# The first four attention steps of an opening: reciprocals on 72 columns, spread back by fp32 matmuls, in a new order

## The chip, the cores and the metric

The kernel runs on one core of one Trainium2 chip. The metric is the device time of one execution in microseconds (us), taken as the median of several runs. The engines are called by the names of the profile: PE (TensorE, matmuls), PEld (its weight loads), DVE (VectorE), ACT (ScalarE), POOL (GpSimd) and SP (SyncE, which issues DMAs).

## What is computed

Sliding-window attention over 8 batches of 8 heads, 576 positions, head size 64, and then a two-layer feed-forward network on all 4608 tokens.

```python
scores = q @ k.T / sqrt(64);  scores = where(|i - j| <= 32, scores, -1e9)
attn = softmax(scores);       x = (attn @ v)            # heads joined: 4608 x 512
h = x @ w_in                                            # 512 -> 2048
out = maximum(0.01 * h, h) @ w_out                      # 2048 -> 512
```

Inputs and output are float32; the matmuls run on bfloat16 copies.

## The kernel before

Attention is cut into 64 steps. Step i is batch i // 8, half (i // 4) % 2 of the positions (288 queries) and head pair i % 4: two heads lie in partitions 0 to 63 and 64 to 127. One step goes through these helpers:

- `score(i)`: PE multiplies keys and queries block by block into the PSUM tile `ps` (columns 224 to 799).
- `exps(i)`: ACT takes the exponential of `ps` into `e` (bfloat16, 576 columns). There is no subtraction of a maximum.
- `masked(i, eng)`: `eng` multiplies by the window's mask into `prob`.
- `sums(i)`: PE multiplies by `ones_bd`, a block matrix of ones, so that each of the 64 rows of a head holds the same sum of probabilities for each of the 288 queries, in the PSUM tile `s`.
- `inverse(i)`: DVE takes the reciprocal of `s` (128 x 288, float32) into SBUF.
- `product(i)`: PE multiplies values and probabilities into the PSUM tile `x`.
- `scaled(i)`: DVE multiplies `x` by the reciprocal into `xT`, the transposed input of the feed-forward network.

The feed-forward network follows group by group (a group is 288 tokens, that is, four steps). `h_tile`, `h_open`, `h_chunk` and `h_first` compute 128 rows of the hidden layer (L401), ACT applies the leaky rectifier into `gT` (L412), and `o_tile` multiplies by `w_out` (L459) and stores 128 tokens.

PSUM is full: four slots of the pool `mmps` (transposes and feed-forward tiles share them), two banks for `ps`, one for `s` and one for `x`.

The order of the instructions on each engine is the order in which the program issues them; each engine runs its own list in order, and the framework adds the waits that data and buffers need. From step 8 on, a planner (`spend`, `due`, `SECOND`) puts attention steps between the matmuls of the feed-forward network. The opening, which is the first batch (steps 0 to 7) and the hidden tiles of its first group, is an order written out by hand (L524 to L649). In it the keys and queries are transposed by PE (`transpose_first`) and copied out of PSUM by `evict_first`; `value_first` casts the first values; `spread` copies the window mask into place, `fill` zeroes the columns of `ps` that no block writes, and `keep_busy` issues matmuls of zeros into columns 0 to 223 of `ps`. The weights `w_in` and `w_out` and the second batch's keys and queries come by DMAs that POOL issues (`load_w_in`, `load_w_out`, `load_first`), which also cast them. After the opening come `h_first(1)`, the other hidden tiles of group 1 (64 matmuls in all), and then the first output tile, ahead of which the planner's first entry transposes the second batch's first keys (`second_keys(0)`, `second_keys(1)`).

Before the change the first steps run as: `masked(0)`, `masked(1)` on DVE and the other six masks on POOL; every `inverse` on 288 columns; `h_chunk(0)` to `h_chunk(2)` (12 matmuls of the first four hidden tiles) stand before or beside `sums(4)`.

Of the kernel before, what the change touches and what calls it, by code (L numbers as in the profile page):

```python
# [16 lines left out]
def kernel(  # L17
# [91 lines left out]
    def load_v(b, p, engs=(nc.sync, nc.sync)):  # L109

        cast = engs[0] is nc.gpsimd
        if not cast:
            vf[b, p] = fload.tile([128, NB, D], FP32, name=f"vf{p}")
        for a, r in enumerate(HEADS):
# [14 lines left out]
    ones_bd = const.tile([128, 128], BF16)  # L129


    zero = const.tile([128, 1], BF16)

    WIN = [
        [((0, 0, 48), (2, 48, 64), (4, 112, 32)), ((1, 16, 64), (3, 80, 64))],
# [41 lines left out]
    nc.vector.memset(zero, 0.0)  # L177
# [24 lines left out]
    def transpose_first(b, p, which):  # L202

        src = (q0b, k0b)[which == "k"]
        tp = mmps.tile([128, ROW, 64], BF16, name="tp", tag="mm")
        for c in range(ROW):
            for r in HEADS:
                nc.tensor.transpose(tp[r, c], src[r, p, c], ident[r, r])  # L208
        trans[b, p, which] = tp.rearrange("p c i -> p i c")

    def evict_first(b, p, which, eng):
        if which == "q":
            if b not in qT:
                qT[b] = attn.tile([128, NPAIR, S], BF16, name="qT")
            to = qT[b][:, p]
        else:
            to = kTs[b, p] = kt.tile([128, S], BF16, name="kT")
        copy_to(eng, to.rearrange("p (i c) -> p i c", c=ROW), trans.pop((b, p, which)))

    def value_first(b, p, eng):  # L220
        copy_to(eng, v0b[:, p], vf[b, p])

    def fill(eng):
        eng.memset(ps[:, 512:512 + HALF], 0.0)
# [48 lines left out]
    def score(i):  # L273
        b, hf, p = where(i)
        if b == 0:
            by_n = ps[:, P0:P0 + 2 * HALF].rearrange("p (n t) -> p n t", n=2)
            for n_, blocks in enumerate(WIN[hf]):
                for blk, i0, n in blocks:
                    lo, hi = 2 * i0, 2 * (i0 + n)
                    for r in HEADS:  # L280
                        nc.tensor.matmul(  # L281
                            by_n[r, n_, lo:hi], kTs[b, p][r, 64 * blk:64 * blk + 64],
                            qT[b][r, p, hf * HALF + lo:hf * HALF + hi], start=True, stop=True,
                        )
        elif b < NATURAL:
            by_n = ps[:, P0:P0 + 2 * HALF].rearrange("p (n t) -> p n t", n=2)
            for n_, blocks in enumerate(WIN[hf]):
                for blk, i0, n in blocks:
                    lo, hi = 2 * i0, 2 * (i0 + n)
                    nc.tensor.matmul(  # L290
                        by_n[:, n_, lo:hi], kbd[b % 2][:, p, blk],
                        qT[b][:, p, hf * HALF + lo:hf * HALF + hi], start=True, stop=True,
                    )
        else:
            by_c = qT[b][:, p].rearrange("p (c i) -> p c i", c=2)
            for n_, blocks in enumerate(WIN[hf]):
                for blk, i0, n in blocks:
                    nc.tensor.matmul(  # L298
                        ps_v[:, n_, :, i0:i0 + n], kbd[b % 2][:, p, blk],
                        by_c[:, :, hf * EVEN + i0:hf * EVEN + i0 + n], start=True, stop=True,  # L300
                    )
        if b > 0:
            exps(i)
            masked(i, nc.vector if i in ON_DVE else nc.gpsimd)

    def exps(i):
        e = attn.tile([128, 2 * HALF], BF16, name="e")
        nc.scalar.activation(out=e, in_=ps[:, P0:P0 + 2 * HALF], func=AF.Exp, scale=scale)  # L308
        probs[i] = e

    def masked(i, eng):
        b, hf, p = where(i)
        e = probs[i]
        pr = prob[:, i % NPROB]
        allowed = mask_first[hf] if b < NATURAL else mask[hf].rearrange("p n c i -> p n (c i)")
        eng.tensor_mul(  # L316
            pr.rearrange("p n c i -> p n (c i)"), e.rearrange("p (n t) -> p n t", n=2), allowed,
        )
        probs[i] = [pr, None, None, None]

    def join(i):
# [4 lines left out]
        nc.vector.tensor_add(both, pr[:, 0], pr[:, 1])  # L326
        probs[i][1] = both

    def sums(i):

        b, hf, p = where(i)
        pr, both = probs[i][:2]
        s = xps.tile([128, HALF], FP32, name="s")
        if both is not None:
            nc.tensor.matmul(s, ones_bd, both, start=True, stop=True)  # L335
        else:
            for n in range(2):
                nc.tensor.matmul(
                    s, ones_bd, pr[:, n].rearrange("p c i -> p (c i)"),
                    start=(n == 0), stop=(n == 1),  # L340
                )
        probs[i][2] = s
        if b > 0:
            inverse(i)

    def inverse(i):
        r = recip.tile([128, HALF], FP32, name="r")
        nc.vector.reciprocal(r, probs[i][2])  # L348
        probs[i][2] = r

    def product(i):

# [73 lines left out]
    def h_close(f):  # L426
        h_out(0, f, opened.pop(f))
# [39 lines left out]
    def keep_busy(t, lo, n, start=False):  # L467


        for _ in range(n):  # L470
            nc.tensor.matmul(
                t[:, lo:lo + 224], ones_bd, busy, start=start, stop=False,
                skip_group_check=True,
            )
# [48 lines left out]

    V, G, A = nc.vector, nc.gpsimd, nc.scalar  # L524
    qT[0] = attn.tile([128, NPAIR, S], BF16, name="qT")
    keep_busy(ps, 0, 14, True)
    fill(V)
    transpose_first(0, 0, "k")
    evict_first(0, 0, "k", V)
    transpose_first(0, 0, "q")  # L530
    evict_first(0, 0, "q", A)
    transpose_first(0, 1, "k")
    score(0)
    evict_first(0, 1, "k", V)
    spread(A, GAP + 32, 2)
    load_v(0, 1, (G, G))
    transpose_first(0, 1, "q")
    exps(0)
    value_first(0, 0, V)
    transpose_first(0, 2, "k")  # L540
    evict_first(0, 1, "q", A)
    spread(V, 0, 3)
    masked(0, V)
    load_v(0, 2, (G, G))
    transpose_first(0, 2, "q")
    evict_first(0, 2, "k", V)
    sums(0)
    evict_first(0, 2, "q", A)
    score(1)
    inverse(0)  # L550
    transpose_first(0, 3, "k")
    exps(1)
    load_v(0, 3, (G, G))
    transpose_first(0, 3, "q")
    evict_first(0, 3, "k", A)
    score(2)
    product(0)
    evict_first(0, 3, "q", A)
    load_w_in(0, 512)
    masked(1, V)  # L560
    exps(2)
    scaled(0)
    sums(1)
    load_w_in(512, 1024)
    score(3)
    inverse(1)
    product(1)
    masked(2, G)
    exps(3)
    score(4)  # L570
    masked(3, G)
    exps(4)
    scaled(1)
    sums(2)
    product(2)
    inverse(2)
    score(5)
    load_w_in(1024, 1536)
    exps(5)
    masked(4, G)  # L580
    score(6)
    scaled(2)
    sums(3)
    h_chunk(0)
    load_w_in(1536, 2048)
    exps(6)
    inverse(3)
    h_chunk(1)
    masked(5, G)
    score(7)  # L590
    product(3)
    h_chunk(2)
    load_w_out(0)
    scaled(3)
    sums(4)
    exps(7)
    h_chunk(3)
    inverse(4)
    masked(7, G)
    product(4)  # L600
    h_close(0)
    h_close(1)
    h_open(4)
    load_w_out(1)
    h_close(2)
    h_open(5)
    scaled(4)
    h_close(4)
    sums(5)
    masked(6, G)  # L610
    h_open(6)
    h_close(3)
    inverse(5)
    h_close(5)
    h_open(7)
    h_close(6)
    product(5)
    load_w_out(2)
    h_close(7)
    h_open(8)  # L620
    h_open(9)
    load_w_out(3)
    h_close(8)
    scaled(5)
    sums(6)
    h_close(9)
    h_open(10)
# [4 lines left out]
    inverse(6)  # L632
    product(6)
    h_close(10)
    h_open(11)
    h_open(12)
    h_close(11)
    h_open(13)
    h_close(12)
    scaled(6)  # L640
    sums(7)
    h_close(13)
    h_open(14)
    inverse(7)
    h_open(15)
    h_close(14)
    product(7)
# [122 lines left out]
```

## Time and profile before

| what | value |
|---|---|
| runs | 317.68, 317.73, 318.78 us; median 317.73 |
| profiled execution | 319.02 us; span from its first to its last instruction 317.3 us |
| mean granted PE clock | 0.984 |
| busy | PE 306.0 (96%), DVE 218.9 (69%), POOL 187.7 (59%), ACT 167.5 (53%), PEld 204.6 (64%) |
| moved by DMA | 46.09 MB, mean 145 GB/s |
| 64 reciprocals on DVE (L348) | 125.2 us, 1956 ns each |
| hidden layer matmuls (L401) | 135.0 us, 1024 of them |
| output matmuls (L459) | 129.5 us |

Busy time is the time in which an engine has at least one instruction running; matmuls are pipelined, so the duration of one is longer than the distance from one to the next. In a timeline a line is a run of like instructions: start, length, engine, source line, operation, tiles, shapes, count, and in brackets the idle time before it with what ended it.

### The profile page before, as it was taken

How to read it: one execution, taken by the hardware profiler on the slowest of the kernel's cores; microseconds unless marked ns; L12 is line 12 of the kernel's file. 1: busy time of each engine (PE TensorE's matmuls, PEld its weight loads, DVE VectorE, ACT ScalarE, POOL GpSimd, SP SyncE). 2: the span in 40 equal slices, each digit the busy share in tenths (PEclk: the TensorE clock that was granted, in tenths of full speed). 3: DMA queues.
4: the chain of work that ended last, by engine and by line, in shares of the span. 5: the costliest groups of instructions: out<-in, count | busy, mean ns of one | idle time of the engine just before them, and what ended most of it. 6: DMA issues, size and time to landing. Idle time of an engine off the chain costs nothing.

```text
span 317.3 us, 6932 instructions
## 1 busy us (share of the span) xinstructions
PE 306.0 (96%) x2692; PEld 204.6 (64%) x2714; DVE 218.9 (69%) x267; ACT 167.5 (53%) x370; POOL 187.7 (59%) x258
## 2 busy tenths in 40 slices
PE   5889999999999999999999999999999999999996
PEld 4657755674755858585765858576765858576653
DVE  2879758699765996788655997688755988565100
ACT  2636755472743828274652828375552837464531
POOL 8989984536356866686546866686647866330000
PEclk9579999999999999999999999999999999999999
DMA  7999999969997994499635995599733450000102
GB/s 130 136 183 207 206 144 237 200 157 235 223 193 184 213 215 118 100 241 208 149 74 152 212 229 134 75 225 232 163 76 107 110 68 35 34 35 1 66 24 77
DMA packets 107313, 46.09 MB, mean 145 GB/s; under 512 B 68752, under 2 KB 102800, under 8 KB 107280
## 3 DMA queue, kind: packets, MB, share of 16 engines
q1 hardware_dynamic: 91936, 37.91, 58.3%
q0 software_dynamic: 14752, 7.59, 18.1%
q8 instruction: 21, 0.34, 0.5%
q10 hardware_dynamic: 592, 0.15, 0.2%
q14 instruction: 12, 0.10, 0.1%
HBM read 36.70 MB, written 9.44 MB: 145 GB/s over the span
## 4 chain that ended last, share of the span: by engine, by line
PE 77%; POOL 10%; DVE 5%; DMA 4%; issue 2%; ACT 1%; SPq 0%; DVEq 0%; ACTq 0%; POOLq 0%
PE mm L459 33%; PE mm L401 33%; PE x L371 4%; PE ps L298 3%; DVE r L348 2%; DMA kf<-in_k_dram 2%; POOL vbd L657 2%; PE s L335 2%; POOL vbd L116 2%; DMA qb<-in_q_dram 2%; POOL prob L316 2%; POOL kb L99 1%; POOL qb L99 1%; PE ps L281 1%; DVE both L326 1%
## 5 line engine op out<-in xcount | busy, mean ns | idle before, releaser
L348 DVE RECIPROCAL r<-s 128x288 f32<-128x288 f32 x64 | 125.2, 1956 | 53.3 <-PE s L335 50.7
L401 PE MATMUL mm<-xT,w_in_bf 128*128 128x288 bf16 x1024 | 135.0, 288 | 0.1
L459 PE MATMUL mm<-w_out_bf,gT 128*128 128x512 bf16 (+2 forms) x570 | 129.5, 373 | 1.3 <-issue 0.2
L412 ACT ACTIVATE gT<-mm 128x288 bf16<-128x288 f32 x256 | 101.5, 410 | 27.1 <-PE mm L401 10.3
L401 PEld LDWEIGHTS <-w_in_bf 128*128 128x128 bf16 x1024 | 98.6, 98 | 25.7 <-issue 0.5
L316 POOL TENSOR_TENSOR prob<-e,mask 128x576 bf16<-128x576 bf16 x48 | 61.3, 1278 | 83.8 <-issue 40.7
L459 PEld LDWEIGHTS <-gT 128*128 128x128 bf16 x592 | 55.8, 98 | 58.0
L464 ACT ACTIVATE o_sb<-mm 128x512 f32<-128x512 f32 (+2 forms) x37 | 21.7, 586 | 91.1 <-PE mm L459 91.1
L308 ACT ACTIVATE e<-ps 128x576 bf16<-128x576 f32 x64 | 41.4, 647 | 17.9 <-PE ps L298 7.4
L387 DVE TENSOR_TENSOR xT<-x,r 128x288 bf16<-128x288 f32 x64 | 29.2, 457 | 7.1 <-PE x L363 0.9
L235 POOL CAST vbd<-vf 64x576 bf16<-64x576 f32 x48 | 33.1, 690 | 1.4
L262 DVE COPY kbd<-kT 64x576 bf16<-64x576 bf16 x48 | 31.2, 650 | 0.3
L230 POOL CAST kb<-kf 96x384 bf16<-96x384 f32 x48 | 27.1, 590 | 1.8 <-DMA kf<-in_k_dram 1.8
L230 POOL CAST qb<-qf 96x384 bf16<-96x384 f32 x48 | 24.4, 535 | 4.4 <-DMA qf<-in_q_dram 3.9
L326 DVE TENSOR_TENSOR both<-prob 128x288 bf16<-128x288 bf16 x52 | 21.7, 417 | 3.2 <-POOL prob L316 2.5
L371 PE MATMUL x<-prob,vbd 128*128 128x96 bf16 (+1 forms) x280 | 22.6, 212 | 0.6 <-DVE xT L387 0.6
L371 PEld LDWEIGHTS <-vbd 128*128 128x128 bf16 x280 | 18.0, 98 | 3.8 <-DVE xT L387 0.7
L298 PEld LDWEIGHTS <-kbd 128*128 128x128 bf16 x240 | 15.5, 98 | 6.9
L298 PE MATMUL ps<-qT,kbd 128*128 128x128 bf16 (+2 forms) x240 | 19.3, 212 | 0.0
L335 PE MATMUL s<-both,ones_bd 128*128 128x288 bf16 x52 | 14.9, 286 | 0.2
L316 POOL TENSOR_TENSOR prob<-e,wide 128x576 bf16<-128x576 bf16 x8 | 10.2, 1276 | 5.3 <-ACT e L308 5.1
L141 ACT ACTIVATE qT<-tp 128x576 bf16<-128x576 bf16 x7 | 4.5, 649 | 7.4 <-PE tp L208 7.4
(51 smaller groups left out, 110.4 us busy)
## 6 DMA issues: line engine op xcount, KB each, us to landing
out_dram<-o_sb SPq DMA_DIRECT2D x35, 256.0 KB, 3.9
vf<-in_v_dram SPq DMA_DIRECT2D x49, 144.0 KB, 3.5
qf<-in_q_dram SPq DMA_DIRECT2D x24, 288.0 KB, 4.3
kf<-in_k_dram SPq DMA_DIRECT2D x24, 288.0 KB, 4.7
w_in_bf<-in_moe_w_in_dram POOLq DMA_DIRECT2D x4, 512.0 KB, 8.1
w_out_bf<-in_moe_w_out_dram POOLq DMA_DIRECT2D x4, 512.0 KB, 8.8
kb<-in_k_dram POOLq DMA_DIRECT2D x4, 144.0 KB, 4.6
qb<-in_q_dram POOLq DMA_DIRECT2D x4, 144.0 KB, 4.8
```

The source lines that it names most:

```text
L230: nc.gpsimd.tensor_copy(out=dst[:, p, 3 * c:3 * c + 3], in_=by_c[c])
L235: nc.gpsimd.tensor_copy(out=vbd[b % 2][r, p, :, r], in_=vf[b, p][r])
L262: nc.vector.tensor_copy(out=to.rearrange("p n (m c) -> p n c m", c=2), in_=kT[r].rearrange("p (c n m) -> p n c m", c=2, n=NB),)
L298: nc.tensor.matmul(ps_v[:, n_, :, i0:i0 + n], kbd[b % 2][:, p, blk], by_c[:, :, hf * EVEN + i0:hf * EVEN + i0 + n], start=True, stop=True,)
L308: nc.scalar.activation(out=e, in_=ps[:, P0:P0 + 2 * HALF], func=AF.Exp, scale=scale)
L316: eng.tensor_mul(pr.rearrange("p n c i -> p n (c i)"), e.rearrange("p (n t) -> p n t", n=2), allowed,)
L348: nc.vector.reciprocal(r, probs[i][2])
L371: nc.tensor.matmul(x[:, lo:hi] if b < NATURAL else x_v[:, :, i0:i0 + n], vbd[b % 2][:, p, blk, :], flat[:, n_, lo:hi] if b < NATURAL else ...
L387: nc.vector.tensor_mul(place(i), x, r)
L401: nc.tensor.matmul(h[:, 0:HALF], w_in_bf[:, c, ts(f, 128)], xT[:, c, ds(g * HALF % RING, HALF)], start=(c == 0), stop=(c == DMC - 1),)
L412: nc.scalar.activation(out=to, in_=x, func=AF.Prelu, alpha=0.01)
L459: nc.tensor.matmul(o[:, lo:hi], gT[:, f, ds(128 * j % RING, 128)], w_out_bf[:, f, lo:hi], start=(f == 0), stop=(f == FFC - 1),)
```

## The change

1. In steps 0 to 3 (`COMPACT`) the 288 columns of sums are put on 72. `pick[:, j]` is a weight matrix that gives the sums of both heads for the j-th quarter (72 queries) on 16 rows per head; eight matmuls, two halves of the window for each of four quarters, accumulate into one 128 x 72 block. The reciprocal is taken of that block. `spread_back` then multiplies it, in float32, by four matrices `back[:, j]` (the transposes of `pick`, divided by 16, made once by `backs`), which puts the reciprocals back on 128 rows and 288 columns of PSUM.
2. Because one operand of `scaled` is now the spread reciprocal in PSUM, the product is copied to SBUF first (`saved`, on DVE for step 0 and on ACT for steps 1 to 3).
3. The sums, the two small blocks and the spread reciprocals are columns of one PSUM tile, `s_all` (128 x 512 float32, one bank).
4. All masks are made on DVE.
5. The hand-written order is a new one, and 15 further calls of `keep_busy` with 1 to 6 matmuls each stand in it; the first call has 11 matmuls instead of 14. The first values are cast on ACT, the window mask is spread on DVE alone, and the copies of the first and last keys have changed engines. The loads keep their order in POOL's queue, which holds no masks between them any more.

```diff
+    CHUNKS = 4
+    PART = HALF // CHUNKS
+    pick = kbd[0][:, 0, 0:CHUNKS]
+    back = const.tile([128, CHUNKS, 128], FP32)
...
+    nc.vector.memset(pick, 0.0)
+    for a, r in enumerate(HEADS):
+        at = pick[r, 0, 16 * a:16 * a + 16]
+        nc.vector.memset(bass.AP(at.tensor, at.offset, [at.ap[0], [160, CHUNKS], [1, 16]]), 1.0)
...
+    s_all = xps.tile([128, 512], FP32, name="s")
+    COMPACT = (0, 1, 2, 3)
+
     def sums(i):
...
-        s = xps.tile([128, HALF], FP32, name="s")
-        if both is not None:
+        s = s_all[:, 0:HALF]
+        if i in COMPACT:
+            s = s_all[:, HALF + i % 2 * PART:HALF + (i % 2 + 1) * PART]
+            for j in range(CHUNKS):
+                for n in range(2):
+                    nc.tensor.matmul(
+                        s, pick[:, j], pr[:, n].rearrange("p c i -> p (c i)")[:, ts(j, PART)],
+                        start=(j == 0 and n == 0), stop=(j == CHUNKS - 1 and n == 1),
+                    )
+        elif both is not None:
             nc.tensor.matmul(s, ones_bd, both, start=True, stop=True)
...
     def inverse(i):
-        r = recip.tile([128, HALF], FP32, name="r")
+        n = PART if i in COMPACT else HALF
+        r = recip.tile([128, n], FP32, name="rc" if i in COMPACT else "r")
         nc.vector.reciprocal(r, probs[i][2])
         probs[i][2] = r
+
+    def backs():
+
+        t = mmps.tile([128, CHUNKS, 128], BF16, name="tp", tag="mm")
+        for j in range(CHUNKS):
+            nc.tensor.transpose(t[:, j], pick[:, j], ident)
+        nc.scalar.activation(out=back, in_=t, func=AF.Copy, scale=1.0 / 16)
+
+    def spread_back(i):
+
+        s = s_all[:, 0:HALF]
+        for j in range(CHUNKS):
+            nc.tensor.matmul(s[:, ts(j, PART)], back[:, j], probs[i][2], start=True, stop=True)
+        probs[i][2] = s
+
+    def saved(i, eng):
+
+        x = joined.tile([128, HALF], FP32, name="x")
+        copy_to(eng, x, probs[i][3])
+        probs[i][3] = x
```

The new order up to the fifth reciprocal, written several calls to a line (`kb(n)` for `keep_busy(ps, 0, n)`, `T(p, "k")` and `E(p, "k", V)` for `transpose_first` and `evict_first` of batch 0; V is DVE, A is ACT, G is POOL):

```python
kb(11, True); backs(); fill(V); value_first(0, 0, A); kb(5); T(0, "k"); E(0, "k", A); kb(3); T(0, "q"); E(0, "q", A)
spread(V, GAP + 32, 2); kb(4); T(1, "k"); spread(V, 0, 3); score(0); E(1, "k", V); exps(0); load_v(0, 1, (G, G))
kb(6); T(1, "q"); masked(0, V); E(1, "q", A); kb(2); product(0); T(2, "k"); saved(0, V); score(1); load_v(0, 2, (G, G))
sums(0); E(2, "k", V); exps(1); T(2, "q"); E(2, "q", A); kb(2); T(3, "k"); masked(1, V); load_v(0, 3, (G, G)); inverse(0)
kb(2); score(2); T(3, "q"); E(3, "k", V); exps(2); spread_back(0); sums(1); E(3, "q", A); masked(2, V); load_w_in(0, 512)
inverse(1); kb(3); score(3); product(1); load_w_in(512, 1024); scaled(0); sums(2); exps(3); spread_back(1); inverse(2)
load_w_in(1024, 1536); saved(1, A); score(4); masked(3, V); product(2); exps(4); load_w_in(1536, 2048); scaled(1)
kb(1); sums(3); saved(2, A); score(5); masked(4, V); spread_back(2); load_w_out(0); exps(5); inverse(3); product(3)
load_w_out(1); scaled(2); saved(3, A); kb(2); score(6); masked(5, V); kb(1); spread_back(3); exps(6); load_w_out(2)
product(4); scaled(3); score(7); load_w_out(3); masked(6, V); kb(1); sums(4); exps(7); h_chunk(0); inverse(4)
h_chunk(1); h_chunk(2); h_chunk(3); masked(7, V); h_close(0); kb(1); sums(5); scaled(4); ...
```

After that the hidden tiles of group 0, steps 5 to 7 and the second batch's loads follow as before, with small shifts. The code from `make_mask(0, nc.gpsimd)` on is unchanged.

More of the change, by code (lines that the diff above doesn't have):

```diff
@@ L107, with load_v @@
     HEADS = (slice(0, 64), slice(64, 128))
-    def load_v(b, p, engs=(nc.sync, nc.sync)):
+    def load_v(b, p, engs=(nc.sync, nc.sync), behind=None):
         cast = engs[0] is nc.gpsimd
@@ L113, in load_v @@
             vf[b, p] = fload.tile([128, NB, D], FP32, name=f"vf{p}")
+            if behind is not None:
+                behind.memset(vf[b, p][0:1, 0, 0:1], 0.0)
         for a, r in enumerate(HEADS):
@@ L129 @@
     ones_bd = const.tile([128, 128], BF16)
-    zero = const.tile([128, 1], BF16)
     WIN = [
@@ L525 @@
     qT[0] = attn.tile([128, NPAIR, S], BF16, name="qT")
-    keep_busy(ps, 0, 14, True)
+    keep_busy(ps, 0, 11, True)
+    backs()
     fill(V)
+    value_first(0, 0, A)
+    keep_busy(ps, 0, 5)
     transpose_first(0, 0, "k")
-    evict_first(0, 0, "k", V)
+    evict_first(0, 0, "k", A)
+    keep_busy(ps, 0, 3)
     transpose_first(0, 0, "q")
     evict_first(0, 0, "q", A)
+    spread(V, GAP + 32, 2)
+    keep_busy(ps, 0, 4)
     transpose_first(0, 1, "k")
+    spread(V, 0, 3)
     score(0)
@@ L534 @@
     evict_first(0, 1, "k", V)
-    spread(A, GAP + 32, 2)
+    exps(0)
     load_v(0, 1, (G, G))
+    keep_busy(ps, 0, 6)
     transpose_first(0, 1, "q")
-    exps(0)
-    value_first(0, 0, V)
+    masked(0, V)
+    evict_first(0, 1, "q", A)
+    keep_busy(ps, 0, 2)
+    product(0)
     transpose_first(0, 2, "k")
-    evict_first(0, 1, "q", A)
-    spread(V, 0, 3)
-    masked(0, V)
+    saved(0, V)
+    score(1)
     load_v(0, 2, (G, G))
+    sums(0)
+    evict_first(0, 2, "k", V)
+    exps(1)
@@ L545 @@
     transpose_first(0, 2, "q")
-    evict_first(0, 2, "k", V)
-    sums(0)
     evict_first(0, 2, "q", A)
-    score(1)
+    keep_busy(ps, 0, 2)
+    transpose_first(0, 3, "k")
+    masked(1, V)
+    load_v(0, 3, (G, G))
     inverse(0)
-    transpose_first(0, 3, "k")
-    exps(1)
-    load_v(0, 3, (G, G))
+    keep_busy(ps, 0, 2)
+    score(2)
     transpose_first(0, 3, "q")
-    evict_first(0, 3, "k", A)
-    score(2)
-    product(0)
+    evict_first(0, 3, "k", V)
+    exps(2)
+    spread_back(0)
@@ L558 @@
+    sums(1)
     evict_first(0, 3, "q", A)
+    masked(2, V)
     load_w_in(0, 512)
-    masked(1, V)
-    exps(2)
-    scaled(0)
[L563 to L568, printed above, removed]
+    inverse(1)
+    keep_busy(ps, 0, 3)
+    score(3)
+    product(1)
+    load_w_in(512, 1024)
+    scaled(0)
+    sums(2)
     exps(3)
+    spread_back(1)
+    inverse(2)
+    load_w_in(1024, 1536)
+    saved(1, A)
     score(4)
-    masked(3, G)
+    masked(3, V)
@@ L572 @@
+    product(2)
     exps(4)
+    load_w_in(1536, 2048)
     scaled(1)
-    sums(2)
-    product(2)
-    inverse(2)
+    keep_busy(ps, 0, 1)
+    sums(3)
+    saved(2, A)
     score(5)
-    load_w_in(1024, 1536)
+    masked(4, V)
+    spread_back(2)
+    load_w_out(0)
     exps(5)
-    masked(4, G)
+    inverse(3)
+    product(3)
+    load_w_out(1)
+    scaled(2)
+    saved(3, A)
+    keep_busy(ps, 0, 2)
     score(6)
[L582 to L585, printed above, removed]
+    masked(5, V)
@@ L586 @@
+    keep_busy(ps, 0, 1)
+    spread_back(3)
     exps(6)
-    inverse(3)
-    h_chunk(1)
-    masked(5, G)
+    load_w_out(2)
+    product(4)
+    scaled(3)
     score(7)
[L591 to L594, printed above, removed]
+    load_w_out(3)
+    masked(6, V)
+    keep_busy(ps, 0, 1)
     sums(4)
     exps(7)
+    h_chunk(0)
+    inverse(4)
+    h_chunk(1)
+    h_chunk(2)
     h_chunk(3)
-    inverse(4)
-    masked(7, G)
-    product(4)
+    masked(7, V)
     h_close(0)
+    keep_busy(ps, 0, 1)
@@ L602 @@
+    sums(5)
+    scaled(4)
     h_close(1)
+    keep_busy(ps, 0, 1)
     h_open(4)
-    load_w_out(1)
     h_close(2)
+    inverse(5)
     h_open(5)
-    scaled(4)
+    h_close(3)
+    product(5)
     h_close(4)
-    sums(5)
-    masked(6, G)
     h_open(6)
-    h_close(3)
-    inverse(5)
     h_close(5)
@@ L616 @@
     h_close(6)
-    product(5)
-    load_w_out(2)
+    scaled(5)
+    keep_busy(ps, 0, 1)
+    sums(6)
     h_close(7)
     h_open(8)
+    inverse(6)
     h_open(9)
-    load_w_out(3)
     h_close(8)
[L624 to L627, printed above, removed]
     load_first(1, 0, "k", 2)
@@ L631 @@
     load_first(1, 2, "q", 2)
-    inverse(6)
+    h_open(10)
+    h_close(9)
+    h_open(11)
+    h_close(10)
     product(6)
-    h_close(10)
-    h_open(11)
+    sums(7)
+    h_close(11)
+    scaled(6)
     h_open(12)
-    h_close(11)
+    inverse(7)
     h_open(13)
     h_close(12)
-    scaled(6)
-    sums(7)
+    h_open(14)
     h_close(13)
-    h_open(14)
-    inverse(7)
     h_open(15)
```

1 line of the change is left out of this document (removed).

## The prediction

> **What bounds the kernel now.** I read the stretches first: busy time of each engine and the granted clock, cut where the clock changes (columns: start and end, length, then PE, PEld, DVE, ACT, POOL busy, the clock, DMA share, GB/s).
>
> ```profile
> 8.40:15.10 6.70, 5.83 (x132) 4.41 (x126) 5.35 (x9) 4.06 (x8) 6.19 (x9) 0.50 1.49 129
> 15.20:18.50 3.30, 1.74 (x40) 1.13 (x37) 3.20 (x3) 1.86 (x3) 3.14 (x4) 1.00 1.20 192
> 18.70:21.90 3.20, 3.20 (x26) 1.86 (x25) 2.66 (x3) 0.65 (x1) 3.18 (x4) 0.50 1.09 161
> 22.10:40.60 18.50, 18.25 (x184) 13.30 (x178) 14.37 (x17) 12.44 (x32) 17.51 (x22) 1.00 1.23 206
> ...
> 80.00:314.40 234.40, 233.53 (x1832) 156.30 (x1846) 158.23 (x187) 126.41 (x285) 129.13 (x170) 1.00 0.64 133
> ```
>
> From 22 us to the last matmul at 314.4 PE hardly pauses. What the opening saves or loses is therefore the shift of the point where the fixed list begins: the transposes of the second batch, which open the first output tile. The PE timeline has that point.
>
> ```profile
> 19.61 2.13 PE L401 MATMUL mm<-xT,w_in_bf 128*128 128x288 bf16 x8
> ...
> 32.40 8.30 PE L401 MATMUL mm<-xT,w_in_bf 128*128 128x288 bf16 x64
> 40.63 0.76 PE L208 MATMUL tp<-ident,kb 64*64 64x64 bf16 x36
> ```
>
> It is at 40.63 us. What sets it? The DVE timeline: from 11.5 us DVE goes from reciprocal to scaling and back.
>
> ```profile
> 11.47 1.96 DVE L348 RECIPROCAL r<-s 128x288 f32<-128x288 f32 x1 [0.60 <-PE s L338]
> ...
> 13.93 0.46 DVE L387 TENSOR_TENSOR xT<-x,r 128x288 bf16<-128x288 f32 x1 [0.20 <-PE x L363]
> ...
> 22.52 0.46 DVE L387 TENSOR_TENSOR xT<-x,r 128x288 bf16<-128x288 f32 x1 [0.70 <-PE x L363]
> 23.35 1.96 DVE L348 RECIPROCAL r<-s 128x288 f32<-128x288 f32 x1 [0.38 <-PE s L338]
> ```
>
> Scaling 0 ends at 14.39, scaling 3 at 22.98, the fifth reciprocal (step 4) starts at 23.35, and 17.28 us later the second batch begins. I compare these three marks. One more view decides much, the waits of the first 48 us, and with it two rows of groups by form:
>
> ```profile
> DVE ps L224 <- PE ps L471: 1.0, 1, 1.0
> ```
>
> ```profile
> L316 POOL TENSOR_TENSOR prob<-e,wide 128x576 bf16<-128x576 bf16 x6 | 7.7, 1278 | 1.9 <-ACT e L308 1.7
> ...
> L316 DVE TENSOR_TENSOR prob<-e,wide 128x576 bf16<-128x576 bf16 x2 | 0.9, 426 | 0.1
> ```
>
> The memset of L224 writes columns 512 to 799 of ps, the zero matmuls columns 0 to 223; it waited 1.0 us all the same. So a wait in PSUM goes by more than the columns touched: I take it by tile.
>
> **The change, part by part.** *Small reciprocals.* 288 columns take 1957 ns, 6.8 ns each; 72 columns are at least 0.49 us and at most the old 1.96; I take 0.54, near the proportional end, because DVE's smallest rows (memsets, 59 ns) leave little that is fixed. Four steps free 4 x 1.42 = 5.7 us of DVE.
>
> *Masks.* Six move from POOL (1.28 us each) to DVE (0.43 each): DVE +2.6, POOL -7.7. POOL then issues its weight loads and the second batch's loads without pauses. That is worth nothing while PE comes later than they land: the second batch's two key loads were issued at 27.85 and 29.26 us and landed 11.9 us later in the median and 12.7 at the latest, so 11.1 and 12.7: the first at 39.0, before 40.63. If PE came sooner than 39.0, this cover would be gone and only what DMA gains would count.
>
> *Sums on few columns.* Two matmuls of 288 columns become eight of 72 with their own weights. The nearest row is the second batch's scores: 5 matmuls of 64 to 128 columns in 0.40 us, each alone 0.2, so 0.05 apart. Eight: 0.40 us, and 0.2 until the last one is out; before, 0.42 in all.
>
> *Spreading.* Four fp32 matmuls of 72 columns per step, f us each. No row shows fp32 on PE. Below: f = 0.05, as the bf16 row. Above: 0.38, a weight load (98 ns) and a 288-column matmul (286 ns) with nothing overlapped. I take 0.22: the load not hidden, and then the 0.122 at which 288-column matmuls follow each other (8.30 us less 0.28, over 64, is 0.125), because 72 columns of fp32 should stand nearer to a pipelined row than to an isolated one.
>
> The Trainium skill, "FP8 and Floating Point Precision", TensorE Precision Notes, says that true fp32 takes four passes through the array. Four passes at the bf16 row's 0.05 would make f = 0.20 and the sum below 0.2 us smaller; no run here shows fp32 on PE.
>
> *The new waits.* Sums, small reciprocals, spread sums and scaling now share one PSUM tile of one bank (s_all), so by the tile rule each waits for the one before: sums(i+1) and spread(i) on PE, then inverse(i+1), a mask and scaled(i) on DVE, then PE again. Before, s had its own bank and was free as soon as the reciprocal had read it, and the reciprocal's copy r lay in SBUF. Behind a waiting sum or spread on PE stand the next score and product, so ACT's exp waits as well.
>
> The Trainium skill, "PSUM — Partial Sum Buffer", PSUM bank collisions, asks for guards by bank and quadrant, not by address. By that rule the wait on s_all cannot be loosened to columns; the row of L224 agrees, and goes further, since its two writers were in different banks.
>
> One period, scaling to scaling: PE 0.40 + 4f + 0.2, DVE 0.54 + 0.43 + 0.46, two handovers of 0.05 (the gap between an exp's end and the score behind it): 2.1 + 4f. Before, 8.59 us from scaling 0 to scaling 3, 2.86 each, some of it cold clock. So the change breaks even per step only at f = 0.19.
>
> *Start of the chain.* Score 0 can start at 7.55 as before; its exp no longer stands behind the spread of the mask on ACT: 8.0 instead of 8.36. But six zero matmuls on ps stand after it and by the tile rule wait for it: 8.65 plus 6 x 0.19 (2.80 us for 14 at the cold clock, 0.2 each) is 9.8, and only then the second head pair's query transposes (8.07 before). Transposes 0.69, ACT copy 0.65, then score 1 behind product 0 and the third keys: about 11.4 against 11.36. From there: exp 1 at 12.1, exp 2 at 14.0 (13.67 before), mask 2 at 14.7, inverse 1 at 15.1, scaling 0 from 15.65 to 16.1. It stands behind these in the new DVE list; before it ended at 14.39: +1.7.
>
> *Steps 0 to 3.* Two full periods, then scaling 3, whose spread has no sums beside it (4f + 0.2 + 0.46 + 0.1 = 4f + 0.8), but score 6 (0.3) and three zero matmuls (0.3) ahead of it on PE's list: 2 x (2.1 + 4f) + 4f + 1.4 = 5.6 + 12f = 8.2. Scaling 3 ends at 24.3; sums 4 take 0.45: the fifth reciprocal at 24.8 instead of 23.35, +1.45.
>
> *After it.* Before, 12 of the 64 matmuls of the first hidden tiles were done by 23.35; now all stand behind sums(4). 12 x 0.125 = +1.5, of which about 0.5 lies in PE's old pauses while DVE finished: +1.0. The last four reciprocals stay 1.96 each and go beside these matmuls as before. ACT's added copies (three of 0.65, three of 0.41) fit into its idle 6.6 us before L141.
>
> Sum: +1.45 + 1.0 = +2.45, the second batch at 43.1. The profiled execution took 319.02 us (span 317.3, 1.7 around it), 1.3 more than the median 317.73; the shift goes on the median: **320.2 us**. With f = 0.05 it would be +0.4, with 0.38 +4.4.
>
> **The rivals.** *Faster: warm clock and waits by column.* Zero matmuls before 8.4 us keep the clock up from there to 15.1, and the fillers and sums wait for nothing outside their columns. Price: six fillers 0.6 less, query transposes 0.22 (0.69 to 0.47), product, transposes and score 0.7; a period that overlaps sums with scaling, 0.5 less, twice; f = 0.05, 2.0 less: 2.45 - 4.5 = -2.1, but PE must not come before the keys at 39.0 (-1.6), except as far as POOL's free queue brings them forward (DMA fell to 134 GB/s at 20 to 22 us against 206 later, 0.7 us). About 315.7. It decides where f is under 0.1 and the fillers don't wait. For it: DVE does lose 3 us of work. Against it: L224's wait, and PE was busy 4.68 of the first 8.3 us and yet went cold.
>
> The Trainium skill, "TensorE: Matmul & The Clock Gate", Part 1, has the clock rise after a busy window of about 3.4 us and fall after an idle one; the four stretches above agree in length (6.8, 3.4, 3.4). By it the fillers alone are worth the 1.5 us of this rival's first part.
>
> *No change.* f near 0.1 and half of the clock gain: 2.45 - 1.4 - 0.8 = +0.2, 318.0.
>
> *Slower still: unpipelined fp32 and a cold stretch.* f = 0.38 (+1.9) and PE cold again in two periods, because it stands waiting for DVE half of the time as in 15.2 to 18.5 (busy 1.74 of 3.30, then cold): PE's part of a period, 1.5 us, doubles in one of them: +1.5. In all +5.9, 323.6.
>
> **How the numbers follow.** My case (f from 0.12 to 0.3, +1.2 to +3.4) 0.48; slower still 0.19; no change 0.20; faster 0.13. The kernel's runs spread over 1.1 us, so 0.5%, 1.6 us, is about what can be told from no change. Of my case a small part, 0.04, falls within it: faster 0.13, same 0.24, slower 0.63. The range takes in my case, no change and half of the outer two: 316.2 to 323.2.
>
> **What would show it.** Right: spread matmuls near 0.2 us apart; small reciprocals of 0.5 us, each beginning only after the spread of the step before; fillers after exp 0; scaling 3 ending at 24 or later; the x36 transposes at about 43. Wrong: the x36 transposes before 40.6; sums on s_all starting while scaling reads it; a clock of 1.00 from 8.4 to 22; transposes of the second batch waiting for DMA, which would mean that PE got there too early.

## The result, and the profile after

The kernel after takes 320.91 us (median of 5 runs, 320.32 to 321.17), the kernel before 317.8 beside it (317.68 to 318.78): a ratio of 1.0087, 95% interval 1.0068 to 1.0107. It is slower by 3.1 us. The profiled execution took 320.94 us, span 319.2, 1.9 more than the profiled one of before. The kernel after ran at a mean granted clock of 1.00 in all of its runs, the kernel before at 1.00 in about half of them (median 317.7 in every later comparison) and at 0.984 to 0.995 in the others (median 318.5 to 319.1), and its profile, 319.02 us, is one of the latter.

The stretches of the kernel after (columns: start and end, length, then PE, PEld, DVE, ACT, POOL busy, the clock, DMA share, GB/s):

```profile
5.40:42.50 37.10, 34.79 (x534) 27.19 (x534) 23.44 (x38) 21.26 (x48) 29.39 (x43) 1.00 1.30 185
...
80.00:316.20 236.20, 235.35 (x1841) 157.29 (x1854) 160.13 (x188) 126.43 (x285) 130.76 (x173) 1.00 0.63 134
```

The cold stretches of before (8.4 to 15.1 and 18.7 to 21.9 us) are gone. PE hardly pauses later on, as before, so the cost again lies ahead of the second batch's transposes. The PE timeline has them, two spreads on the way, and the fillers behind score 0:

```profile
8.16 0.41 PE L289 MATMUL ps<-qT,kT 64*64 64x96 bf16 x10
9.31 0.73 PE L511 MATMUL ps<-busy,ones_bd 128*128 128x224 bf16 x6 [0.74 <-ACT e L316]
...
13.99 1.11 PE L382 MATMUL s<-rc,back 128*128 128x72 f32 x8
14.94 0.42 PE L349 MATMUL s<-prob,kbd 128*128 128x72 bf16 x8
...
19.80 1.11 PE L382 MATMUL s<-rc,back 128*128 128x72 f32 x8
...
23.68 0.41 PE L357 MATMUL s<-prob,ones_bd 128*128 128x288 bf16 x2
23.92 2.12 PE L441 MATMUL mm<-xT,w_in_bf 128*128 128x288 bf16 x16
...
34.32 8.31 PE L441 MATMUL mm<-xT,w_in_bf 128*128 128x288 bf16 x64
42.56 0.76 PE L216 MATMUL tp<-ident,kb 64*64 64x64 bf16 x36
```

They start at 42.56 instead of 40.63. In every profile of this case, whatever the version, the device time is 278.38 to 278.44 us more than this start, so the mark carries the whole difference; a median of 317.7 stands for transposes at about 39.3 (an estimate by that distance). Four fp32 matmuls appear as eight weight loads and eight matmuls; the next matmul follows 0.95 to 1.04 us after the first of them. The fillers write columns 0 to 223 of ps, which exp 0 does not read, and wait for it all the same. The DVE timeline shows what DVE does with the time that it saves:

```profile
15.93 0.40 DVE L427 TENSOR_TENSOR xT<-x,s 128x288 bf16<-128x288 f32 x1
17.76 0.61 DVE L368 RECIPROCAL rc<-s 128x72 f32<-128x72 f32 x1 [1.44 <-PE s L382]
...
20.95 0.61 DVE L368 RECIPROCAL rc<-s 128x72 f32<-128x72 f32 x1 [1.55 <-PE s L382]
...
23.14 0.46 DVE L427 TENSOR_TENSOR xT<-x,s 128x288 bf16<-128x288 f32 x1 [0.91 <-PE s L382]
...
24.12 1.96 DVE L368 RECIPROCAL r<-s 128x288 f32<-128x288 f32 x1 [0.16 <-PE s L357]
```

Four small reciprocals take 2.4 us in place of 7.8, but from the first scaling to the fifth reciprocal DVE waits 3.9 us for spreads (1.44, 1.55, 0.91). Two of these waits are of a reciprocal, which reads other columns of s_all than the spread writes. Scaling 0 ends at 16.33, scaling 3 at 23.60; the fifth reciprocal starts at 24.12, 0.77 us after that of before, and the transposes come 18.44 us behind it, 1.16 us more than before. These are differences to a profile with cold stretches; the experiment with fillers alone, below, gives them at a clock that did not fall.

### The profile page after: what moved, and what is told of

It is laid out like the page before. It is cut to its first block, busy times and chain, and to the rows that moved or that the text cites. A ratio compares the mean times of both kernels' runs of the same rounds, so it can differ in the third digit from the quotient of the medians.

```text
span 319.2 us, 7124 instructions
## 1 busy us (share of the span) xinstructions
PE 310.3 (97%) x2784; PEld 210.0 (66%) x2806; DVE 215.7 (68%) x276; ACT 169.9 (53%) x374; POOL 180.0 (56%) x252
## 3 DMA queue, kind: packets, MB, share of 16 engines
q0 software_dynamic: 14752, 7.59, 18.0%
## 4 chain that ended last, share of the span: by engine, by line
PE 74%; DMA 11%; POOL 6%; DVE 4%; issue 4%; SPq 1%; ACT 0%; POOLq 0%; DVEq 0%; ACTq 0%
PE mm L499 33%; PE mm L441 32%; DMA qb<-in_q_dram 5%; DMA w_in_bf<-in_moe_w_in_dram 4%; PE x L411 4%; PE ps L306 3%; PE s L354 2%; DMA kf<-in_k_dram 2%; DVE r L368 2%; POOL v0b L118 1%; POOL prob L324 1%; DVE both L334 1%; POOL qb L99 1%; POOL w_in_bf L558 1%; POOL kb L99 1%
## 5 line engine op out<-in xcount | busy, mean ns | idle before, releaser
L368 DVE RECIPROCAL r<-s 128x288 f32<-128x288 f32 x60 | 117.3, 1956 | 51.9 <-PE s L354 50.7
L441 PE MATMUL mm<-xT,w_in_bf 128*128 128x288 bf16 x1024 | 133.3, 286 | 0.1
L427 DVE TENSOR_TENSOR xT<-x,r 128x288 bf16<-128x288 f32 x60 | 27.4, 457 | 6.4 <-PE x L403 0.7
L511 PE MATMUL ps<-busy,ones_bd 128*128 128x224 bf16 x46 | 8.6, 305 | 2.8 <-DVE ones_bd L185 1.5
L721 POOL MEMSET vbd<- 128x1152 bf16 x8 | 8.0, 1047 | 0.0
```

The lines of the kernel that those rows point to most:

```text
L427: nc.vector.tensor_mul(place(i), x, r)
L441: nc.tensor.matmul(h[:, 0:HALF], w_in_bf[:, c, ts(f, 128)], xT[:, c, ds(g * HALF % RING, HALF)], start=(c == 0), stop=(c == DMC - 1),)
```

## The experiments

My theory: the loss is the fp32 spreads and the alternation that s_all forces on PE and DVE, then hidden-layer work that PE does too late. Rivals: the masks on DVE; the fillers; the order alone, whatever the reciprocals; and the clock as the hidden difference.

**The spread in a bank of its own**, on the kernel after:

```diff
     def spread_back(i):
-        s = s_all[:, 0:HALF]
+        s = mmps.tile([128, 512], FP32, name="mm", tag="mm")[:, 0:HALF]
```

> The changed kernel with the spread reciprocals written to a free slot of the transposes' PSUM pool instead of s_all. Theory (PE and DVE take turns because sums, small reciprocals, spread and scaling share one bank): the next step's sums and small reciprocal no longer wait for the scaling before; scaling 3 ends about 1.3 us sooner than 23.6, the second batch's transposes start near 41.1 instead of 42.56, time about 319.4. Rival (only the price of the fp32 matmuls counts, four at 0.22 us per step on PE): nothing moves, 320.9.

320.59 us (320.21 to 320.81, 6 runs), ratio to before 1.0074 (1.0053 to 1.0096), transposes at 42.08. The DVE timeline:

```profile
19.11 0.61 DVE L368 RECIPROCAL rc<-s 128x72 f32<-128x72 f32 x1
20.58 0.46 DVE L427 TENSOR_TENSOR xT<-x,mm 128x288 bf16<-128x288 f32 x1 [0.86 <-PE mm L382]
...
22.66 0.46 DVE L427 TENSOR_TENSOR xT<-x,mm 128x288 bf16<-128x288 f32 x1 [1.25 <-PE mm L382]
23.64 1.96 DVE L368 RECIPROCAL r<-s 128x288 f32<-128x288 f32 x1 [0.15 <-PE s L357]
```

The waits of the reciprocals for spreads are gone, so those waits were the shared tile's (the edit changes the tile and the bank together): the fourth small reciprocal comes at 19.11 instead of 20.95. But it buys 0.3 us only; of the 0.48 us at the transposes, 0.23 is an earlier start of score 0 in this trace (7.93 instead of 8.16). The scalings now wait 0.86 and 1.25 us for the spread itself. Spread 2 stands in PE's list behind a filler that waits 0.50 us for the exp before, sums and the next score; spread 3 behind a product, three fillers and a score. One wait turned into another; the shared bank as the main cause falls.

**The spread in bf16**, on the kernel after (the reciprocals and `back` are rounded to bf16):

```diff
-    back = const.tile([128, CHUNKS, 128], FP32)
+    back = const.tile([128, CHUNKS, 128], BF16)
...
-        r = recip.tile([128, n], FP32, name="rc" if i in COMPACT else "r")
+        r = recip.tile([128, n], BF16 if i in COMPACT else FP32, name="rc" if i in COMPACT else "r")
```

> The changed kernel with back and the small reciprocals in bf16 (they are rounded to bf16), so the spread is four bf16 matmuls per step. Theory: 0.05 instead of 0.24 us each, 12 of them in the chain, so 2.1 us less: scaling 3 ends near 21.5, the second batch starts near 40.4, time 318.8. Rival (the turns of PE and DVE with their handovers cost, not fp32): under 0.7 us, 320.2 or more.

318.81 us (318.05 to 320.73, 12 runs), ratio 1.002 (1.0002 to 1.0038): 2.1 us less than after. The PE timeline:

```profile
14.35 0.30 PE L383 MATMUL s<-rc,back 128*128 128x72 bf16 x4
14.48 0.43 PE L349 MATMUL s<-prob,kbd 128*128 128x72 bf16 x8
...
40.64 0.76 PE L216 MATMUL tp<-ident,kb 64*64 64x64 bf16 x36
```

A spread of 0.95 us becomes one of 0.13 us (start to the next matmul's start), and the transposes come 1.92 us sooner. In this trace score 0 even comes 0.35 us later (8.51), so the shift that the spreads account for is rather larger. This is the largest single mend that was found: 2.1 of the 3.1 us.

**The new order with full reciprocals**, on the kernel after:

```diff
-    COMPACT = (0, 1, 2, 3)
+    COMPACT = ()
...
-    spread_back(0)
```

and the other three calls of `spread_back` likewise.

> The changed kernel with COMPACT empty: full sums and reciprocals of 288 columns in all steps, no spread, all else (order, fillers, masks on DVE, copies of the products) as changed. Theory (the new order is made for short reciprocals and puts masks and copies on DVE): slower than the change by 1 to 2 us, 322.4, scaling 0 at 17.5, the second batch at 44. Rival (the compact sums and their spread are the loss and the order is good): faster than the change, 318 to 319.

323.61 us (323.49 to 324.11, 4 runs), ratio 1.0173 (1.0146 to 1.02), the fifth reciprocal at 26.13. So the small reciprocals do gain in this order, 2.7 us even with their fp32 spreads (some of that is the clock, 0.983 to 0.989 here). It is the rest of the change that they have to pay for; which part of it (order, masks, copies), this run does not show.

**The masks alone**, on the kernel before: the six masks of POOL on DVE.

```diff
-    masked(2, G)
+    masked(2, V)
```

and 3 to 7 likewise.

> The kernel before with its six POOL masks on DVE and nothing else. Theory (before, DVE's chain of reciprocals bounds the opening, and each 0.43 us mask lies in it unless it fits a wait): 0.8 to 1.5 us slower than before, about 318.9. Rival (masks hide in DVE's waits, and POOL's loads come sooner): no change or faster, 317.8 or less.

319.49 us (318.0 to 321.36, 12 runs), ratio 1.004 (1.0018 to 1.0063). At clock 1.00 it takes 318.15 (3 runs), 0.4 more than before at that clock; the other 9 runs take 319.9, 1.0 more than the runs of before whose clock fell (318.9, 8 of 23). In before the masks lie in DVE's chain and cost something, but less than their 2.6 us of DVE time. Why the clock fell in more of the runs stays open.

**Without the fillers**: the kernel after less its 15 added calls of `keep_busy`.

```diff
-    keep_busy(ps, 0, 6)
```

and the other 14 likewise.

> The changed kernel without the 15 added calls of zero matmuls (the first 11 stay). Theory (the fillers keep PE's clock up in the opening; the exp they wait for costs less): the granted clock falls to 0.5 somewhere between 8 and 26 us in most runs, time 321.5 to 322.5. Rival (the fillers only stand in the way of the transposes and sums behind them): 320.3 or less, 0.6 us saved at the six after exp 0.

321.24 us (320.87 to 321.63, five runs; a sixth took 327.78), ratio 1.0094 (1.0068 to 1.0119). The PE timeline shows the clock in the transposes' duration (the kernel after has 0.47 from 6.09 us on):

```profile
12.07 0.69 PE L216 MATMUL tp<-ident,qb 64*64 64x64 bf16 x18
...
13.75 0.47 PE L216 MATMUL tp<-ident,qb 64*64 64x64 bf16 x18
```

The fillers do warm the clock. What they bring net of their own cost is 0.3 us by the medians and 0.5 by the means of five runs each, little more than their scatter, and the two profiles have the transposes at 42.48 and 42.56; both the theory (a clock that falls, 321.5 or more) and the rival (320.3 or less) missed. The recorded clock does not tell this: it is 1.00 in all six runs, and from 4 to 12 us of this profile, where the transposes take 0.69. A mean of 1.00 says that the clock did not fall, not that it was up from the start. The Trainium skill, "TensorE: Matmul & The Clock Gate", Part 1, has a busy window of about 3.4 us raise the clock; by the durations in this trace it rose between 12.6 and 13.5 us, after some 8 us in which PE worked in bursts (busy 2.00 us of the time from 4 to 8 us, 3.24 from 8 to 12).

**Without the six fillers behind score 0** alone:

```diff
-    keep_busy(ps, 0, 6)
```

> The changed kernel without the one call of six zero matmuls behind exp 0. Theory (they wait for the exp by the tile rule and hold the second pair's query transposes): those transposes start 1.3 us sooner (8.7 instead of 9.97), of which 0.5 or less reaches the second batch, because the third keys come later; 320.4. Rival (the clock needs them): a clock under 1.00 and 321 or more.

320.21 us (319.84 to 321.77, 9 runs), ratio 1.006 (1.004 to 1.008): 0.7 us less than after by the medians, so these six cost more than they bring. That it is by the wait for exp 0 shown above is argued: the profile is of the slowest run (321.77, clock 0.993), in which the keys ahead of score 0 came 0.8 us later (their transposes at 8.66 instead of 7.85).

**Fillers alone**, on the kernel before: 5, 3, 6 and 3 ahead of the transposes of the first keys, first queries, second keys and third keys.

```diff
+    keep_busy(ps, 0, 5)
     transpose_first(0, 0, "k")
```

> The kernel before with four calls of zero matmuls (5, 3, 6 and 3) ahead of the first key, first query, second key and third key transposes, nothing else. Theory (the spread of its runs, 317.4 to 319.6, goes by whether the clock stays up): all runs at a clock of 1.00, median 317.5, highest under 318.2. Rival (fillers that wait for exp 0 and delay transposes): 318.2 or more.

318.99 us (317.84 to 320.69, 12 runs), ratio 1.0017 (0.9997 to 1.0038). Only 3 of 12 runs kept the clock at 1.00 (317.86): early fillers do not hold it, my expectation fell. The profiled run, one of the three, shows what caps a faster opening:

```profile
39.46 0.76 PE L208 MATMUL tp<-ident,kb 64*64 64x64 bf16 x36 [0.79 <-DMA kb<-in_k_dram]
```

The second batch's keys land only then; without this wait the transposes would come at 38.67. At a clock that does not fall the keys, not the reciprocals, set the end here, and by its time (317.7, that is, transposes at about 39.3) probably in before too, of which no such run was profiled.

This profile is the nearest to the kernel before at the clock of the kernel after, and it shows where the 3.1 us lie. Its DVE timeline:

```profile
13.32 0.45 DVE L387 TENSOR_TENSOR xT<-x,r 128x288 bf16<-128x288 f32 x1
...
21.31 1.96 DVE L348 RECIPROCAL r<-s 128x288 f32<-128x288 f32 x1
```

The kernel after has its fifth reciprocal 2.81 us later (24.12) and 1.08 us more from there to where the transposes could start (18.44 against 17.36); the 0.79 us for which this run waits for keys hides a part: 2.81 + 1.08 - 0.79 = 3.10. The first part is lost at the start: scaling 0 ends at 16.33 instead of 13.77, because its small reciprocal starts at 12.73 (the full one here at 11.14), the spread runs at 13.99 and the scaling stands in DVE's list behind mask 2 and the second small reciprocal. From scaling 0 to scaling 3 the two take about the same, 7.27 and 7.59 us: the fp32 spreads use up what the small reciprocals save there. With bf16 spreads it is 5.10.

**The first hidden chunks late**, on the kernel before: `h_chunk(0)` to `h_chunk(2)` moved behind `sums(4)`, as in the new order.

```diff
     sums(3)
-    h_chunk(0)
...
     exps(7)
+    h_chunk(0)
+    h_chunk(1)
+    h_chunk(2)
     h_chunk(3)
```

> The kernel before with its first three groups of hidden matmuls (12 of 64) moved behind sums(4), where the change has them; nothing else. Theory: PE has 1.5 us more work behind the fifth reciprocal, of which 0.5 fits its pauses, and starts that reciprocal up to 0.5 us sooner: 0.5 to 1.0 us slower, 318.5 to 319. Rival (the matmuls hide beside the reciprocals anyway): 318.0 or less.

320.35 us (318.63 to 321.35, 12 runs), ratio 1.0061 (1.0039 to 1.0082); 318.66 at clock 1.00 (2 runs), 0.9 more than before at that clock; the other ten take 320.4, 1.5 more than the runs of before whose clock fell (318.9). The profile, one of the two, shows the term itself, on DVE and on PE:

```profile
21.82 1.96 DVE L348 RECIPROCAL r<-s 128x288 f32<-128x288 f32 x1
```

```profile
40.28 0.76 PE L208 MATMUL tp<-ident,kb 64*64 64x64 bf16 x36
```

From the fifth reciprocal to the transposes it takes 18.46 us instead of 17.28, like the 18.44 of the kernel after. The tail's term is these chunks, and worth about what the prediction put on it.

**A chunk early, in the kernel after:**

```diff
-    keep_busy(ps, 0, 1)
+    h_chunk(0)
     sums(3)
```

and the seven zero matmuls behind that place left out.

> The kernel after, with the first hidden-layer chunk (four 288-column matmuls) where the single zero matmul ahead of sums(3) stands, in PE's pause of 18.3 to 18.8 us, and without the seven zero matmuls behind that place. Theory (the tail's +1.0 us is work that PE does late: it does not pause any more from 19.8 us on, so every matmul behind that point costs its whole distance): 0.5 us of chunk into the pause and 7 x 0.11 us of fillers away, less what the chunk delays: the second batch's transposes at 41.4 instead of 42.56, 319.7 us. Rival (the opening's DVE chain sets the end, PE's list only follows): the transposes stay within 0.3 us of 42.56, 320.7 us.

321.15 us (320.85 to 321.76, 6 runs), ratio 1.0077 (1.0048 to 1.0107): no gain. The PE timeline, in which score 0 starts at 8.42, 0.26 us later than in that of the kernel after:

```profile
18.52 0.66 PE L441 MATMUL mm<-xT,w_in_bf 128*128 128x288 bf16 x4
19.35 0.42 PE L349 MATMUL s<-prob,kbd 128*128 128x72 bf16 x8 [0.17 <-DVE xT L427]
...
26.37 0.40 PE L357 MATMUL s<-prob,ones_bd 128*128 128x288 bf16 x2 [0.58 <-DVE r L368]
...
42.60 0.76 PE L216 MATMUL tp<-ident,kb 64*64 64x64 bf16 x36
```

The chunk fits the pause: sums(3) comes at 19.35 instead of 19.09, by that start alone. But the work taken out of the tail comes back as a wait of 0.58 us for a full reciprocal, and of the 1.2 us that I expected the trace gains 0.2 from the fifth reciprocal (24.36) to the transposes. The tail is bounded twice, by PE and just behind it by DVE.

**The mends together**: bf16 spreads, no six fillers, none from sums(3) on, `h_chunk(0)` ahead of score(6) and `h_chunk(1)` ahead of score(7).

```diff
-    keep_busy(ps, 0, 2)
+    h_chunk(0)
     score(6)
...
+    h_chunk(1)
     score(7)
```

> The kernel after, with bf16 spreads (the reciprocals and the matrix back rounded to bf16), without the six zero matmuls after score(0) and the seven from sums(3) on, and with the first two hidden-layer chunks ahead of score(6) and score(7). Theory (the losses are the fp32 spreads, the six fillers and late PE work, and they add up): the transposes would come at 42.56 - 2.1 - 0.6 - 1.2 = 38.7 us, but the second batch's keys land at 39.1 to 39.4, so PE waits for a DMA there, as in the kernel before with early fillers: transposes at 39.4, 317.4 to 317.8 us, equal to the kernel before. Rival (the terms overlap, each mend uncovers the next wait): transposes after 40.0 without a DMA wait, 318.2 or more.

318.93 us (318.18 to 321.15, 12 runs), ratio 1.0011 (0.999 to 1.0033). At clock 1.00 it takes 318.46 (8 runs), 0.3 less than bf16 spreads alone (318.79) and 0.8 more than before. The rival holds: the terms do not add up. In 4 of 12 runs the clock fell (1 of 12 with bf16 spreads alone). The profile is of one of them (321.15), and its PE timeline has a wait that is new:

```profile
19.55 1.14 PE L442 MATMUL mm<-xT,w_in_bf 128*128 128x288 bf16 x4 [1.36 <-DMA w_in_bf<-in_moe_w_in_dram]
```

The early chunk stands waiting for its weights, and from 20 to 24 us, behind this wait, the granted clock is 0.50. In the two runs below the same wait is 0.29 and 0.48 us: a chunk this early meets the landing of w_in.

**The keys loaded earlier**, on top of that:

```diff
+    load_first(1, 0, "k", 2)
+    load_first(1, 0, "q", 2)
     load_w_out(2)
```

> The same as e10_mended, with the loads of the second batch's first keys and queries ahead of the third and fourth quarter of w_out in POOL's queue. Theory (in e10_mended the landing of the keys is the bound): the keys land about 5 us sooner, the transposes at 38.7 to 39.0 without a DMA wait, 0.4 to 0.7 us less than e10_mended, about 317.0, faster than the kernel before. Rival (w_out lands later by the same 2.9 us and becomes the bound, or the PE work does): no gain over e10_mended, and a DMA wait at the output matmuls (w_out) in place of the one at the transposes.

318.57 us (318.0 to 320.46, 12 runs), ratio 1.0006 (0.9983 to 1.003); 318.47 at clock 1.00 (10 runs). The keys land at 33.5 instead of 39 us, no output matmul waits for w_out, and nothing is gained. The PE timeline says why:

```profile
21.36 1.14 PE L442 MATMUL mm<-xT,w_in_bf 128*128 128x288 bf16 x8
23.57 0.40 PE L357 MATMUL s<-prob,ones_bd 128*128 128x288 bf16 x2 [1.07 <-DVE r L369]
...
39.80 0.76 PE L216 MATMUL tp<-ident,kb 64*64 64x64 bf16 x36
```

PE does not reach the keys before 39.8: it waits 1.07 us for the fifth reciprocal to read its sums.

**Another order of the tail**, on top of that: mask 7 on POOL, two hidden tiles ahead of sums(5), products 6 and 7 earlier.

```diff
     h_close(0)
+    h_close(1)
+    h_open(4)
+    h_open(5)
     sums(5)
...
     h_open(10)
+    product(6)
```

> The same as e11_mended_keys, with another order behind exp 7 alone: the last mask on POOL, two hidden tiles (8 matmuls, 1.0 us) ahead of sums(5), where PE waited 1.07 us for the fifth reciprocal to read its sums, and product(6) and product(7) six and eight dense matmuls earlier, where DVE waited 0.37 and 0.35 us for them. Theory (what follows the fifth reciprocal is set by DVE's four full reciprocals, the mask among them and two late products; PE's own work there fits beside them): PE's wait is filled, from the fifth reciprocal to the second batch's transposes it takes 17.2 to 17.4 us instead of 18.24, as in the kernel before (17.28), the transposes come at 38.8 to 39.0 without a DMA wait, and the time is 0.9 us less than that of e11_mended_keys: 317.3 to 317.7 us at an even clock. Rival (PE's work alone sets this stretch): no change, transposes at 39.8.

318.11 us (317.66 to 319.6, 12 runs), ratio 1.0011 (0.9995 to 1.0026) to before, which has 317.79 here. The PE timeline:

```profile
21.46 2.42 PE L442 MATMUL mm<-xT,w_in_bf 128*128 128x288 bf16 x16
23.71 0.41 PE L357 MATMUL s<-prob,ones_bd 128*128 128x288 bf16 x2
...
39.66 0.76 PE L216 MATMUL tp<-ident,kb 64*64 64x64 bf16 x36
```

The wait of 1.07 us is filled, yet from the first dense matmul behind sums(4) to the transposes it takes 18.20 us instead of 18.44; I expected 1 us less. PE's own work there (120 dense matmuls at 0.129, that is 8.24 over 64, and three pairs of sums and product at 0.61) is 17.3 us, and several short waits of 0.2 to 0.3 us make up the rest. So the rival, PE's work, is nearer to it. At clock 1.00 the version is 0.4 us behind before (318.10 against 317.67). No version beats the kernel before.

## Why the prediction was right, point by point

- **The time.** 320.2 was forecast, 320.91 measured, slower as forecast. The costs named were the right ones (late start, fp32 spreads, waits by tile, late chunks); the shared bank counted for less than I thought. That the number came so near is partly luck: the shift was forecast 0.5 us above what the two profiles show, and was put on a median 1.3 us below the profile that it was worked out from.
- **Small reciprocals**: 0.54 forecast, 0.605 measured. Masks: 0.43, measured 0.438. Eight sums: 0.40 apart and 0.2, measured 0.42 in all, 0.25 to 0.37 until the next matmul.
- **Spreads**: f = 0.22, measured 0.95 / 4 = 0.24, up to 0.26; the choice nearer to the pipelined row was right. The Trainium skill, "FP8 and Floating Point Precision", TensorE Precision Notes, has true fp32 in four passes; the trace shows two pairs of weight load and matmul for each, 0.12 us apart (what each does inside it does not show), and the estimate of 0.20 by the page is close to the measured price. With bf16 the spread costs 0.13 for four. By the sum's 12 f this would be 12 x (0.24 - 0.03) = 2.5 us; the transposes moved by 1.92, or 2.27 counted from score 0, the time by 2.1.
- **The waits by tile** are there: the fillers wait 0.74 us for exp 0, and two small reciprocals 1.44 and 1.55 us for spreads. That the shared bank is what the period is made of was too strong: with a bank of its own the spread is late in PE's list, and 0.3 us comes back. The step that sized the period as PE's and DVE's work in turn came out near (2.98 forecast, 2.70 and 2.84 measured, by the ends of scaling 0 to 2: 16.33, 19.03, 21.87), and with a bank of its own the three intervals take nearly as long (16.23 to 23.12, that is 6.89 instead of 7.27): PE's list holds nearly the same alternation.
- **The start**: scaling 0 at 16.1 forecast, 16.33 measured; the second head pair's keys, whose transposes stand ahead of score 0, landed later (score 0 at 8.16 instead of 7.55) and the six fillers ran warm (0.66 us until the next matmul instead of 1.15), which offset each other. Over the ten profiles in the new order score 0 starts between 7.37 and 9.16 us, so some tenths between two single traces are no effect.
- **Steps 0 to 3**: 8.2 forecast, 7.27 measured (16.33 to 23.60). Mis-sized term: the last one, from scaling 2 to scaling 3, 4f + 1.4 = 2.28, measured 1.73; the score and fillers ahead of the last spread ran from 21.20 to 21.97, beside the small reciprocal and scaling 2 (done at 21.56 and 21.87), which that spread needed in any case.
- **The tail**: +1.0 forecast, +1.16 measured, and alone 1.18 in the trace. Its working holds for PE: 128 dense matmuls, three pairs and three fillers make 18.6 us, and 18.64 passed from 23.92 to 42.56. It did not say what is late next: DVE's four full reciprocals, 0.6 us behind.
- **The shift and its base**: +2.45 forecast, +1.93 between the two profiles, +3.2 between runs at clock 1.00 (320.91 - 317.72). The step that failed is the base: a profile with two cold stretches was used to work out the shift, and this was put on a median of runs that have them less often. The 1.3 us between that profile and the median was noted and not followed up; the warm clock, which I gave to the rival, then made up for part of it. Against the profile with fillers, at an even clock, the fifth reciprocal is 2.81 us late, not 0.77, and the start alone 2.56: the cold stretches of before had hidden that.
- **The rivals.** "Faster" was right in the clock (1.00 from 5.4 us on) and wrong in its other two conditions, f and the fillers, and POOL's free queue brought the keys no earlier (about 39 us in both: issued at 18.86 instead of 27.85, they landed 20.3 us later instead of 11.2). "No change" fell with f, though the clock's gain came in full. "Slower still" fell with f = 0.24.

What stays open: at clock 1.00 the mended versions keep 0.4 to 0.8 us over before. By the traces the last one loses it mostly behind the fifth reciprocal, 18.00 us (21.66 to 39.66) against 17.36; it has four dense matmuls more there, 0.5 us by the distance above. Ahead of it masks (0.4) and the copies of the products are candidates; I did not test the copies, nor an earlier scaling 0.

## What to carry to other kernels

Cheaper work on the bounding engine counts only if the path through the other engines does not grow: here 5.4 us of DVE time were bought with 0.95 us of fp32 matmuls and two handovers per step, and DVE waited instead; and the first result of the chain came 2.6 us later, which no shorter step behind it made good. Before adding up terms, look for the second limit behind the first: taking work off either one moves the end only up to the other. And cost a change against a profile in the same clock as the runs it is compared with.

## What I had not expected of the hardware

- An fp32 matmul of 128 x 128 by 72 columns runs as two weight loads and two matmuls, 0.24 us in a stream, against 0.03 in bf16.
- The added zero matmuls warm the clock (transposes at 0.47 us from 6.09 us on in the kernel after, only at 13.75 without them), for 0.3 to 0.5 us net in 320, and six of them in a wrong place cost 0.7. The recorded clock is 1.00 in both cases.
- The same kernel differs by 0.8 to 1.4 us between runs at clock 1.00 and at 0.984 to 0.995; the kernel with fillers at 1.00 in every run was the slower one.
